# Sigmoid attention with a token-mixing MLP: 64x64 transposes for a part, PSUM as four pairs, output in half blocks

## The chip, the cores and the metric

The kernel runs on one core of a Trainium2 chip. The metric is the time of one execution on the device, in microseconds; beside it stands the span of the profiled execution, from its first to its last instruction. The engines are named as in the profile: PE is TensorE, DVE is VectorE, ACT is ScalarE, POOL is GpSimd and SP is SyncE, which issues most DMAs.

## The reference

```
# q, k, v: (8, 12, 448, 64) fp32
scores = q @ k^T / 8 - log(448)
attn = sigmoid(scores)
x = (attn @ v), heads side by side        # (8, 448, 768)
wq, wk = x @ w_q, x @ w_k                 # 768 -> 64
W_tok = (wq @ wk^T) / 8                   # (8, 448, 448)
mixed = W_tok @ x
out = relu(mixed) @ w_out                 # (8, 448, 768) fp32
```

The kernel multiplies wk^T by x first, a 64x768 matrix, and then wq by that, so that the 448x448 matrix W_tok is never made.

## The kernel before

**Groups.** The 96 heads are taken four at a time: 24 groups, three for each of the 8 batch elements u. For a group, q, k and v are loaded as fp32 by SyncE (`load1`), 448 KB each, and cast to bf16 by GpSimd (`cast1`). q and k must then stand with the 64 head dimensions on partitions. `tr` does that in one of two ways. For most groups TensorE makes seven whole-array transposes (128x128) for q and seven for k into a PSUM bank, and VectorE copies them out (L161, L165). For the groups in `TWICE`, 16 to 22, q and k are loaded nearly twice over (`qb`, `kb`, four DMAs of 216 KB each), and VectorE transposes them in 32x32 blocks from SBUF to SBUF (L154), without TensorE.

**Attention.** A group has seven score steps (`scores`, S). A step is four matmuls of 64 rows, 64 columns and 448 moving columns, one on each quarter of the array, into a pair of PSUM banks; then ScalarE takes the sigmoid of 128x896 elements (L179). Seven value steps (`values`, P), again four matmuls each, add up the group's output in one pair, which VectorE casts to the tile xt.

**MLP.** For each u: `tr_x` (x, eight whole transposes per group, evacuated to xn), `mlp_wqk` (W, six matmuls into one bank), `mlp_wkn` (N, transposes of wk), `mlp_tmp` (U, eight matmuls of 128x64), `mlp_mix` (M, four matmuls on quarters of the array, then relu). For each pair of u, `out_chunk` (O) makes 14 blocks of 128x384 output from six matmuls of 384 columns each, a copy to SBUF by VectorE (capital O) or ScalarE (small o), and a store.

**PSUM.** Eight banks are handed out by two lists. `free2` has three pairs, for scores, values and mixes; `free1` has two single banks, for everything else. Both are first in, first out, and the next user's first matmul waits until the last one's evacuation is done.

**Order.** TensorE runs in program order, and that order is written out by hand: `PLAN`, one letter for each step. Loads and casts follow the list `ORDER` as far as buffers are free (`pump_loads`, `pump`). A capital K is the second half of group 0's k; each of the 25 strings of `PLAN` but the last holds the seven score steps of a group. The array's shape is 128x128 for whole transposes, W and O, 64x64 for S, P and M, and 128x64 for U.

Of the kernel before, what the change touches and what calls it, by code (L numbers as in the profile page):

```python
# [16 lines left out]
def kernel(  # L17
# [19 lines left out]
    P = 128  # L37
# [27 lines left out]
    ps_f = pool("ps_f", 1, space=bass.MemoryType.PSUM)  # L65

    free2 = ["a", "b", "c"]
    free1 = ["d", "e"]

    def bank2(name):  # L70
        n = free2.pop(0)
        return n, ps_q.tile([P, 2, 512], F32, tag=n, name=name)

    def bank(shape, dtype, name):
        n = free1.pop(0)
        return n, ps_f.tile(shape, dtype, tag=n, name=name)
# [3 lines left out]
    wqk32 = singles.tile([P, NC, P], F32, name="wqk32")  # L80
# [4 lines left out]
    zeros = singles.tile([P, P], BF16)  # L85
# [16 lines left out]
    TWICE = {'q': (16, 17, 18, 19, 20, 21, 22), 'k': (16, 17, 18, 19, 20, 21, 22)}  # L102
# [3 lines left out]

    def load1(n, nm, eng):
        u, j = quads[n]
        if n in TWICE.get(nm, ()):
            t = p_lb.tile([P, 2, 14 * HD], F32, tag=nm + "b32", name=nm + "b32")  # L110
            for g in range(2):
                src = SRC[nm][u, 4 * j + 2 * g : 4 * j + 2 * g + 2].rearrange(
                    "h (p r) d -> p h (r d)", r=14
                )
                for dh in range(2):
                    r0 = 64 * g + 32 * dh
                    eng.dma_start(  # L117
                        out=t[r0 : r0 + 32, :, 0 : 13 * HD + 32],
                        in_=src[:, :, 32 * dh : 32 * dh + 13 * HD + 32],
                    )  # L120
        else:
            t = p_ld.tile([P, 2, NI * HD], F32, tag=nm + "32", name=nm + "32")
            eng.dma_start(  # L123
                out=t,
                in_=SRC[nm][u, 4 * j : 4 * j + 4].rearrange(
                    "(g h) (p i) d -> (h p) g (i d)", g=2, i=NI
                ),
            )
        ld[nm, n] = t

    def cast1(n, nm, eng):
        if n in TWICE.get(nm, ()):
# [5 lines left out]
        else:  # L138
            p = p_v16 if nm == "v" else p_c16
            t16 = p.tile([P, NI, 2, HD], BF16, tag=nm + "16", name=nm + "16")  # L140
            eng.tensor_copy(  # L141
                out=t16.rearrange("p i b d -> p b i d"),
                in_=ld.pop((nm, n)).rearrange("p b (i d) -> p b i d", i=NI),
            )
        ld[nm + "16", n] = t16

    qk = {}

    def tr(n, nm):
        t16 = ld.pop((nm + "16", n))  # L150
        t = p_qk.tile([P, 2, NI, NP], BF16, tag=nm + "t", name=nm + "t")
        qk[nm, n] = t
        if n in TWICE.get(nm, ()):
            nc.vector.transpose(  # L154
                out=t.rearrange("p h i n -> p (h i n)").bitcast(F32),
# [3 lines left out]
        fb, ps = bank([P, NI, 2, NP], BF16, "pt" + nm)  # L159
        for i in range(NI):  # L160
            nc.tensor.transpose(  # L161
                ps[:, i].rearrange("p h n -> p (h n)"),
                t16[:, i].rearrange("p b d -> p (b d)"), ident16,
            )
        nc.vector.tensor_copy(out=t, in_=ps.rearrange("p i h n -> p h i n"))  # L165
        free1.append(fb)
# [3 lines left out]
    def scores(n, i):  # L170
        fb, sc = bank2("sc")
        for g in range(2):
            for h in range(2):
                nc.tensor.matmul(  # L174
                    sc[HALF[h], g, 0:S], qk["k", n][HALF[g], h, i, :],
                    qk["q", n][HALF[g], h].rearrange("p i n -> p (i n)"), start=True, stop=True,
# [3 lines left out]
        free2.append(fb)  # L180
# [4 lines left out]
    def values(n, i, tail):  # L185
        u, j = quads[n]
        if i == 0:
            pv[n] = bank2("pv")
        fb, ps = pv[n]
# [6 lines left out]
        if i == NI - 1:  # L196
# [5 lines left out]
            free2.append(fb)  # L202
# [3 lines left out]
    def tr_x(n, tail):  # L206
# [3 lines left out]
        fb, ps = bank([P, 4, 2, 2, HD], BF16, "px")  # L210
        for h in range(2):
            for m in range(4):
                nc.tensor.transpose(  # L213
                    ps[:, m, :, h], xt(u, j)[:, h, m * P : (m + 1) * P], ident16
                )
        for g in range(2) if tail else (slice(0, 2),):
            w = slice(2 * j * P, 2 * (j + 1) * P) if not tail else slice((2 * j + g) * P, (2 * j + g + 1) * P)
            COPY["s" if tail and g else "v"](  # L218
                out=xns[u][:, :, w],
                in_=ps[:, :, g].rearrange("p m h d -> p m (h d)")  # L220
                if tail else ps.rearrange("p m g h d -> p m (g h d)"),
            )
        free1.append(fb)
# [4 lines left out]
    def mlp_wqk(u, c, tail):  # L228
        if c == 0:
            pw[u] = bank([P, S], F32, "pw")  # L230
        fb, ps = pw[u]
# [3 lines left out]
        if c == NC - 1:  # L235
# [6 lines left out]
            free1.append(fb)  # L242

    def mlp_wkn(u):
        fb, ps = bank([P, 4, P], BF16, "pk")
        for m in range(4):
            nc.tensor.transpose(ps[:, m], wqks[u % 2][:, m * P : (m + 1) * P], ident16)
        wkn[u] = p_one.tile([P, 4, DH], BF16, tag="wkn", name="wkn")
        nc.vector.tensor_copy(out=wkn[u], in_=ps[:, :, 64:128])
        free1.append(fb)  # L250

    def mlp_tmp(u, act):
        tmps[u] = p_one.tile([P, NB], BF16, tag="tmp", name="tmp")
        fb, ps = bank([P, NB], F32, "pt")
# [7 lines left out]
        free1.append(fb)  # L262
# [7 lines left out]
    def mlp_mix(u, c, act, tail):  # L270
        if c == 0 and u % 2 == 0:
            mxs[u // 2] = [p_mx.tile([P, 2, 2, S], BF16, tag=f"mx{n}", name="mx") for n in range(NC // 2)]
        fb, ps = bank2("pm")
# [13 lines left out]
        free2.append(fb)  # L287
# [3 lines left out]

    def out_chunk(act, tail):
        w, m, nb = chunks.pop(0)
        if nb == 0:
# [3 lines left out]
        def block(ps, w0, w1):  # L298
            for c in range(NC):
# [14 lines left out]
        fb, ps = bank([P, NB], F32, "po")  # L314
        if tail and w == NU // 2 - 1 and not chunks:
            h = NB // 2
            block(ps[:, 0:h], NB, NB + h)
            nc.vector.tensor_copy(out=o[:, NB : NB + h], in_=ps[:, 0:h])
            fb2, ps2 = bank2("po")
            block(ps2[:, 0, 0:h], NB + h, D)  # L320
            nc.scalar.copy(out=o[:, NB + h :], in_=ps2[:, 0, 0:h])
            store(slice(NB, NB + h))
            store(slice(NB + h, D))
            return
        block(ps, nb * NB, (nb + 1) * NB)
        COPY["s" if act else "v"](out=o[:, nb * NB : (nb + 1) * NB], in_=ps)  # L326
        free1.append(fb)
# [6 lines left out]
    def load_weights():  # L334
        for x, w in enumerate((moe_w_q, moe_w_k)):
            nc.sync.dma_start(
                out=wqk32[:, :, 64 * x : 64 * x + 64], in_=w.rearrange("(c p) n -> p c n", p=P)
# [20 lines left out]
    nc.vector.memset(zeros, 0.0)  # L358
    nc.vector.memset(bias_t, attn_bias)
    nc.gpsimd.memset(ident, 0.0)  # L360
# [6 lines left out]
    fb, ps = bank2("pwarm")  # L367
    for _ in range(32):
        nc.tensor.matmul(ps[:, 0, 0:P], zeros, zeros, start=True, stop=True)
    free2.append(fb)  # L370
    for t in xts:
        nc.vector.memset(t[:, :, S:], 0.0)
    for t in wqks:
# [4 lines left out]
        "v0 q1 k1 v1 k2 q2 q3 k3 q4 k4 v2 k5 k6 w0 k7 v3 "  # L378
        "w1 q5 q6 k8 v4 w2 q7 w3 v5 w4 k9 q8 v6 q9 w5 w6 "
        "v7 q10 k10 v8 v9 q11 k11 q12 v10 k12 v11 q13 k13 k14 q14 q15 "  # L380
        "v12 q16 k15 v13 v14 q17 k16 v15 k17 q18 k18 q19 v16 k19 v17 k20 "
        "k21 v18 v19 v20 v21 q20 q21 q22 v22 q23 k22 k23 v23 "
# [3 lines left out]
    BACK = {}  # L386
    for nm in "qkv":
        mine = {True: [], False: []}
        for n in range(N):
            kind = n in TWICE.get(nm, ())  # L390
            BACK[nm, n] = (kind, list(mine[kind]))
            mine[kind].append(n)

    def pump_loads():
        while len(loaded) < len(ORDER):
            nm, n = ORDER[len(loaded)]
            if nm == "w":
                if n >= 3 and ("w", n - 2) not in cast:
                    break
                load_wout(n - 1) if n else load_weights()  # L400
            else:
                kind, before = BACK[nm, n]
                back = 2 if kind else 3
# [154 lines left out]
```

## Time and profile before

| | before |
|---|---|
| median of 3 runs | 205.62 us (205.08 to 206.51) |
| the profiled execution | 204.95 us, its span 203.2 us |
| PE (TensorE) busy | 192.2 us, 95% |
| ACT (ScalarE) busy | 171.2 us, 84% |
| DVE (VectorE) busy | 123.1 us, 61% |
| POOL (GpSimd) busy | 80.3 us, 40% |
| first sigmoid of scores starts, last one ends | 6.81 us, 177.69 us |
| HBM read, written | 41.75 MB, 11.01 MB |

In the profile's rows a group of instructions stands with its source line, its engine, the tiles it writes and reads, and the shape. For TensorE, 64\*64 or 128\*128 is the part of the array in use. Matmuls are pipelined: each has a record from its start to its modelled end, and these overlap, so the time that a matmul takes from the next is seen only between starts. "Idle before" names the instruction that ended a wait.

### The profile page before, as it was taken

Reading aid. Unit: us, or ns where it says so; the run is one execution under the profiler, and the core shown is the slowest. Engines: PE = TensorE matmul, PEld = TensorE weight load, DVE = VectorE, ACT = ScalarE, POOL = GpSimd, SP = SyncE. Lnnn points to the kernel's source line nnn. Section 1 sums busy time; section 2 is a strip of 40 time slices with the busy share of each in tenths; the row PEclk is TensorE's granted clock in tenths of the full one; section 3 lists DMA queues with packets and bytes.
Section 4 is the critical chain, followed back from the end, with each engine's and each line's share of the span. In section 5 each row is a group of like instructions: output and inputs, shape, how many; then the busy total and the mean of one; then the engine's idle time right before and its main releaser. Section 6 shows DMA issues by size and latency. Waiting matters only on the chain.

```text
span 203.2 us, 5863 instructions
## 1 busy us (share of the span) xinstructions
PE 192.2 (95%) x2388; PEld 108.6 (53%) x2388; DVE 123.1 (61%) x196; ACT 171.2 (84%) x200; POOL 80.3 (40%) x95
## 2 busy tenths in 40 slices
PE   7669999999999999999999999999999899999991
PEld 7335545545556566555656555545455455555561
DVE  2226655866498567668777776858777654471230
ACT  4796999999989999889999999898998959974511
POOL 1577688676416624217642442511632600000000
PEclk9996999999999999999999999999999999999999
DMA  6999999899998999999999999999899933303575
GB/s 193 374 383 375 325 380 355 245 395 382 380 381 258 331 254 317 223 265 261 247 223 285 256 282 236 367 260 252 258 287 214 345 90 78 80 3 97 152 203 168
DMA packets 27786, 53.13 MB, mean 262 GB/s; under 512 B 4464, under 2 KB 19952, under 8 KB 27760
## 3 DMA queue, kind: packets, MB, share of 16 engines
q1 hardware_dynamic: 26960, 51.19, 85.9%
q10 hardware_dynamic: 800, 1.57, 2.1%
q8 instruction: 18, 0.29, 0.6%
q14 instruction: 8, 0.07, 0.1%
HBM read 41.75 MB, written 11.01 MB: 260 GB/s over the span
## 4 chain that ended last, share of the span: by engine, by line
DMA 41%; PE 31%; SPq 8%; ACT 8%; issue 4%; POOL 4%; DVE 1%; ACTq 1%; POOLq 0%
DMA qb<-in_q_dram 17%; DMA kb<-in_k_dram 12%; PE po L300 11%; PE sc L174 6%; ACT at L179 6%; SPq L117 5%; PE pv L192 5%; DMA q<-in_q_dram 4%; DMA out_dram<-o 4%; DMA v<-in_v_dram 4%; SPq L123 2%; PE pw L232 2%; PE ptk L161 2%; POOL k L134 2%; PE pt L257 2%
## 5 line engine op out<-in xcount | busy, mean ns | idle before, releaser
L179 ACT ACTIVATE at<-sc,bias_t 128x896 bf16<-128x896 f32 x168 | 156.1, 1016 | 13.6 <-PE sc L174 12.7
L300 PE MATMUL po<-wout,mx 128*128 128x384 bf16 (+1 forms) x342 | 61.8, 324 | 0.5 <-ACT o L326 0.3
L174 PE MATMUL sc<-qt,kt 64*64 64x448 bf16 x672 | 57.3, 363 | 2.4 <-DVE kt L451 1.0
L192 PE MATMUL pv<-at,v 64*64 64x448 bf16 x672 | 43.2, 353 | 0.7 <-POOL v L141 0.6
L300 PEld LDWEIGHTS <-mx 128*128 128x128 bf16 x342 | 30.9, 98 | 24.0 <-issue 7.0
L174 PEld LDWEIGHTS <-kt 64*64 64x64 bf16 x672 | 22.1, 104 | 24.3 <-issue 13.0
L201 DVE CAST xt<-pv 128x896 bf16<-128x896 f32 x23 | 25.0, 1088 | 16.1 <-PE pv L192 15.9
L326 DVE COPY o<-po 128x384 f32<-128x384 f32 x39 | 21.7, 556 | 16.9 <-PE po L300 11.8
L141 POOL CAST v<-v 128x896 bf16<-128x896 f32 x24 | 22.4, 934 | 15.2 <-PE pv L192 7.8
L268 DVE TENSOR_SCALAR mx<-pm 128x896 bf16<-128x896 f32 (+1 forms) x24 | 23.0, 969 | 7.2 <-PE pm L277 7.1
L192 PEld LDWEIGHTS <-v 64*64 64x64 bf16 x672 | 20.2, 107 | 12.3 <-issue 2.0
L218 DVE COPY xn<-px 128x1024 bf16<-128x1024 bf16 (+1 forms) x24 | 15.9, 663 | 7.3 <-PE px L213 7.2
L141 POOL CAST q<-q 128x896 bf16<-128x896 f32 x16 | 14.9, 933 | 9.9 <-DMA out_dram<-o 4.4
L141 POOL CAST k<-k 128x896 bf16<-128x896 f32 x16 | 14.9, 933 | 7.1 <-DMA k<-in_k_dram 4.3
L134 POOL CAST k<-kb 128x896 bf16<-128x896 f32 x7 | 8.3, 1192 | 19.4 <-DMA kb<-in_k_dram 9.2
L134 POOL CAST q<-qb 128x896 bf16<-128x896 f32 x7 | 8.2, 1190 | 18.3 <-issue 7.9
L213 PE MATMUL px<-ident,xt 128*128 128x128 bf16 x192 | 14.8, 220 | 0.1
L326 ACT COPY o<-po 128x384 f32<-128x384 f32 x16 | 7.7, 482 | 8.1 <-PE po L300 8.0
L213 PEld LDWEIGHTS <-xt 128*128 128x128 bf16 x192 | 11.5, 98 | 5.6 <-issue 4.8
L165 DVE COPY qt<-ptq 128x896 bf16<-128x896 bf16 x16 | 9.7, 618 | 7.1 <-PE ptq L161 7.0
L232 PE MATMUL pw<-xt,wqk 128*128 128x448 bf16 x48 | 13.8, 356 | 0.0
L165 DVE COPY kt<-ptk 128x896 bf16<-128x896 bf16 x16 | 9.9, 619 | 5.7 <-PE ptk L161 5.5
(53 smaller groups left out, 125.6 us busy)
## 6 DMA issues: line engine op xcount, KB each, us to landing
v<-in_v_dram SPq DMA_DIRECT2D x24, 448.0 KB, 7.8
out_dram<-o SPq DMA_DIRECT2D x47, 192.0 KB, 6.0
q<-in_q_dram SPq DMA_DIRECT2D x17, 448.0 KB, 7.5
k<-in_k_dram SPq DMA_DIRECT2D x16, 448.0 KB, 8.5
qb<-in_q_dram SPq DMA_DIRECT2D x28, 216.0 KB, 6.9
kb<-in_k_dram SPq DMA_DIRECT2D x28, 216.0 KB, 7.4
w<-in_moe_w_out_dram SPq DMA_DIRECT2D x6, 384.0 KB, 7.5
out_dram<-o ACTq DMA_DIRECT2D x7, 192.0 KB, 3.2
```

The source lines that it names most:

```text
L134: eng.tensor_copy(out=t16.rearrange("p h i d y -> p h y i d"), in_=ld.pop((nm, n)).rearrange("p h (y i d) -> p h y i d", y=2, d=HD)[..., 0 ...
L141: eng.tensor_copy(out=t16.rearrange("p i b d -> p b i d"), in_=ld.pop((nm, n)).rearrange("p b (i d) -> p b i d", i=NI),)
L165: nc.vector.tensor_copy(out=t, in_=ps.rearrange("p i h n -> p h i n"))
L174: nc.tensor.matmul(sc[HALF[h], g, 0:S], qk["k", n][HALF[g], h, i, :], qk["q", n][HALF[g], h].rearrange("p i n -> p (i n)"), start=True, st ...
L179: nc.scalar.activation(at, sc[:, :, 0:S], ACTF.Sigmoid, bias=bias_t, scale=attn_scale)
L192: nc.tensor.matmul(ps[HALF[g], h, 0:S], ld["v16", n][HALF[h], i, g, :], ats[n, i][HALF[h], g, :], start=(i == 0), stop=(i == NI - 1),)
L201: nc.vector.tensor_copy(out=xt(u, j)[:, :, 0:S], in_=ps[:, :, 0:S])
L213: nc.tensor.transpose(ps[:, m, :, h], xt(u, j)[:, h, m * P : (m + 1) * P], ident16)
L232: nc.tensor.matmul(ps, wqk16[:, c, :], xt(u, c // 2)[:, c % 2, 0:S], start=(c == 0), stop=(c == NC - 1),)
L268: nc.vector.tensor_scalar(dst, ps, moe_scale, 0.0, ALU.mult, ALU.max)
L300: nc.tensor.matmul(ps, mxs[w][c % 3][:, c // 3].rearrange("p b s -> p (b s)")[:, m * P : (m + 1) * P], wout16[:, c, w0:w1], start=(c == 0) ...
L326: COPY["s" if act else "v"](out=o[:, nb * NB : (nb + 1) * NB], in_=ps)
```

## The change

q, k and v, the casts and the arithmetic stay as they are. What changes:

- **Transposes.** A letter of `PLAN` now says how a group's q and k are transposed: a and b in the whole array, q and k in 64x64 tiles (28 matmuls each for seven), c and d by VectorE. Groups 1 to 8, 10 and 11 are of the first kind, 9, 12 to 15 and 17 of the second, 16 and 18 to 23 of the third. X is a transposition of x in the whole array, x one in 64x64 tiles (32 matmuls for eight): eight X and 16 x. wk is transposed in tiles too. q and k of a group go to one pair of banks and are evacuated by one copy.
- **PSUM.** All eight banks are four pairs. `bank2` gives a pair, `bank1` half of one; `release` joins halves again.
- **Output.** An output block is made in two steps of three matmuls each, with other work between them; of the very last block the two halves of columns are computed, copied and stored one after the other.
- **Fillers.** F is a step of four matmuls on zeros with 512 columns, into the pair that is used next; there are 15.
- **Order.** `PLAN` and `ORDER` are new; w_q and w_k are loaded through the buffers of w_out.

```diff
-    ps_f = pool("ps_f", 1, space=bass.MemoryType.PSUM)
-    free2 = ["a", "b", "c"]
-    free1 = ["d", "e"]
-    def bank2(name):
+    pairs = [ps_q.tile([P, 2, 512], F32, tag=f"pp{n}", name=f"pp{n}") for n in range(4)]
+    pairs16 = [t.rearrange("p b x -> p (b x)").bitcast(BF16).rearrange("p (b x) -> p b x", b=2) for t in pairs]
+    free2 = [0, 1, 2, 3]
+    halves = []
+    def bank2():
         n = free2.pop(0)
-        return n, ps_q.tile([P, 2, 512], F32, tag=n, name=name)
-    def bank(shape, dtype, name):
-        n = free1.pop(0)
-        return n, ps_f.tile(shape, dtype, tag=n, name=name)
+        return n, pairs[n], pairs16[n]
+    def bank1():
+        if halves:
+            n, b = halves.pop(0)
+        else:
+            n, b = free2.pop(0), 0
+            halves.append((n, 1))
+        return (n, b), pairs[n][:, b], pairs16[n][:, b]
+    def release(fb):
+        if isinstance(fb, int):
+            free2.append(fb)
+        elif (fb[0], 1 - fb[1]) in halves:
+            halves.remove((fb[0], 1 - fb[1]))
+            free2.append(fb[0])
+        else:
+            halves.append(fb)
...
-    zeros = singles.tile([P, P], BF16)
+    zeros = singles.tile([P, 512], BF16)
...
-    TWICE = {'q': (16, 17, 18, 19, 20, 21, 22), 'k': (16, 17, 18, 19, 20, 21, 22)}
...
+    PLAN = (
+        "FSSFSFKFFSFSabSSa",
+        "SbFPPSPSPSPFPPSabSFPPSP",
+        "SPabSPPSPFSabSXSSxPPP",
+        "SPPPPSSWWWSXWWSWSabSFF",
+        "SNaSbSUSPPPSMPPPSPSPPPM",
+        "SPPSPPSabSFqkSXSMSab",
+        "SSPPPPSPPPSabSWXSSWWXWP",
+        "SPPPSPPPSoOSqkSOWSWOSo",
+        "SNqkSUSOXSPMPSPPPSPPSOO",
+        "SPPxSPPPSPPSoWOSMSWWWoSFM",
+        "SWOWSFSqkOSNOSPPxSPPPPSP",
+        "SoOSUSPPqSPkPPSPPSWOSPPP",
+        "SPPPPSOWSxSOWMSWWoSMSoWO",
+        "SPPxSPcPPSPPSOOOSMSXOSPPPPNd",
+        "SPPPSUqkSSOXOSScOWOWSx",
+        "SoOWSMSOOSPPPdPSPPPSOOSM",
+        "SWoWoSMSOWOSPPxSPPPNScPPSoO",
+        "SSSoUSOOOSPPMSPPPSPP",
+        "SOOSPPdxSPPPPSPSooooMScSoO",
+        "SOOSPPMSPPPPSPSWWoSdxWoWSx",
+        "SOWOSxSoWScPdPPPPNSPPSUOS",
+        "SMOOoocxSPPMPmPPdPSPSWoWOSSSWoWWWOO",
+        "SNSOOoSxSPPPcPPdSSPPoOUSxPP",
+        "SPPPSPPSOWoWSMSWOoPPSPS",
+        "ooPPPMPMOWOWWoxxNoOooUOoOoMMmOoOooOOooOoOOooOOoo",
+    )
+    PLAN = "".join(PLAN)
+    KIND = ["a"] + [t for t in PLAN if t in "qac"]
...
+    def twice(nm, n):
+        return nm in "qk" and KIND[n] == "c"
...
+    qk = {}
+    ps_qk = {}
+    def transposes(ps, t16, r):
+        for x, i in enumerate(range(r.start, r.stop)):
+            for g in range(2):
+                for h in range(2):
+                    nc.tensor.transpose(
+                        ps[HALF[g], h, x * NP : (x + 1) * NP], t16[HALF[h], i, g, :],
+                        ident16[HALF[h], HALF[h]],
+                    )
+    def transposes_whole(ps, t16, r):
+        for x, i in enumerate(range(r.start, r.stop)):
+            nc.tensor.transpose(
+                ps[:, x * P : (x + 1) * P], t16[:, i].rearrange("p b d -> p (b d)"), ident16,
             )
...
+    def tr(n, nm, kind):
...
+        if kind in "cd":
...
-        fb, ps = bank([P, NI, 2, NP], BF16, "pt" + nm)
-        for i in range(NI):
-            nc.tensor.transpose(
-                ps[:, i].rearrange("p h n -> p (h n)"),
-                t16[:, i].rearrange("p b d -> p (b d)"), ident16,
-            )
-        nc.vector.tensor_copy(out=t, in_=ps.rearrange("p i h n -> p h i n"))
-        free1.append(fb)
+        if t == 0:
+            ps_qk[n] = bank2()
+        fb, _, ps = ps_qk[n]
+        if kind in "ab":
+            transposes_whole(ps[:, t], t16, slice(0, NI))
+        else:
+            transposes(ps[:, :, t * S : (t + 1) * S], t16, slice(0, NI))
+        if t == 1:
+            qk[n] = p_qk.tile([P, 2, 2, NI, NP], BF16, tag="qk", name="qk")
+            if kind in "ab":
+                nc.vector.tensor_copy(
+                    out=qk[n].rearrange("p t h i n -> p t i h n"),
+                    in_=ps[:, :, 0 : 2 * S].rearrange("p t (i h n) -> p t i h n", i=NI, h=2),
+                )
+            else:
+                nc.vector.tensor_copy(
+                    out=qk[n].rearrange("p t h i n -> p t h (i n)"),
+                    in_=ps[:, :, 0 : 2 * S].rearrange("p h (t x) -> p t h x", t=2),
+                )
+            release(fb)
...
-    def tr_x(n, tail):
+    def tr_x(n, tail, whole):
...
-        fb, ps = bank([P, 4, 2, 2, HD], BF16, "px")
-        for h in range(2):
-            for m in range(4):
-                nc.tensor.transpose(
-                    ps[:, m, :, h], xt(u, j)[:, h, m * P : (m + 1) * P], ident16
-                )
+        if whole:
+            fb, _, ps = bank1()
+            ps = ps.rearrange("p (m g h d) -> p m g h d", m=4, g=2, h=2)
+            for h in range(2):
+                for m in range(4):
+                    nc.tensor.transpose(
+                        ps[:, m, :, h], xt(u, j)[:, h, m * P : (m + 1) * P], ident16
+                    )
...
+        fb, _, ps = bank2()
+        for m in range(4):
+            for h in range(2):
+                for g in range(2):
+                    for c in range(2):
+                        nc.tensor.transpose(
+                            ps[HALF[c], g, (2 * m + h) * HD : (2 * m + h + 1) * HD],
+                            xt(u, j)[HALF[g], h, (2 * m + c) * HD : (2 * m + c + 1) * HD],
+                            ident16[HALF[g], HALF[g]],
+                        )
         for g in range(2) if tail else (slice(0, 2),):
...
+        release(fb)
...
     def mlp_wkn(u):
-        fb, ps = bank([P, 4, P], BF16, "pk")
+        fb, _, ps = bank1()
         for m in range(4):
-            nc.tensor.transpose(ps[:, m], wqks[u % 2][:, m * P : (m + 1) * P], ident16)
+            for c in range(2):
+                nc.tensor.transpose(
+                    ps[HALF[c], m * DH : (m + 1) * DH],
+                    wqks[u % 2][HALF[1], (2 * m + c) * DH : (2 * m + c + 1) * DH],
+                    ident16[HALF[1], HALF[1]],
+                )
...
+    opened = []
     def out_chunk(act, tail):
-        w, m, nb = chunks.pop(0)
-        if nb == 0:
+        if opened:
+            w, m, nb, fb, ps = opened.pop()
+            part = 1
+        else:
+            w, m, nb = chunks.pop(0)
+            fb, ps, _ = bank1()
+            part = 0
...
-        def block(ps, w0, w1):
-            for c in range(NC):
+        def block(ps, w0, w1, c0, c1):
+            for c in range(c0, c1):
...
-        fb, ps = bank([P, NB], F32, "po")
-        if tail and w == NU // 2 - 1 and not chunks:
+        last = w == NU // 2 - 1 and not chunks
+        if last:
             h = NB // 2
-            block(ps[:, 0:h], NB, NB + h)
-            nc.vector.tensor_copy(out=o[:, NB : NB + h], in_=ps[:, 0:h])
-            fb2, ps2 = bank2("po")
-            block(ps2[:, 0, 0:h], NB + h, D)
-            nc.scalar.copy(out=o[:, NB + h :], in_=ps2[:, 0, 0:h])
-            store(slice(NB, NB + h))
-            store(slice(NB + h, D))
+            c0 = NB + part * h
+            block(ps[:, 0:h], c0, c0 + h, 0, NC)
+            COPY["vs"[part]](out=o[:, c0 : c0 + h], in_=ps[:, 0:h])
+            release(fb)
+            store(slice(c0, c0 + h))
+            if not part:
+                opened.append((w, m, nb, *bank1()[:2]))
             return
-        block(ps, nb * NB, (nb + 1) * NB)
+        ps = ps[:, 0:NB] if not part else ps
+        block(ps, nb * NB, (nb + 1) * NB, part * NC // 2, (part + 1) * NC // 2)
+        if not part:
+            opened.append((w, m, nb, fb, ps))
+            return
...
     def load_weights():
+        w32["qk"] = p_w32.tile([P, D], F32, tag="w32", name="w32")
...
-    nc.vector.memset(zeros, 0.0)
+    nc.vector.memset(zeros[:, 0:P], 0.0)
     nc.vector.memset(bias_t, attn_bias)
+    nc.vector.memset(zeros[:, P:], 0.0)
...
-        "v0 q1 k1 v1 k2 q2 q3 k3 q4 k4 v2 k5 k6 w0 k7 v3 "
-        "w1 q5 q6 k8 v4 w2 q7 w3 v5 w4 k9 q8 v6 q9 w5 w6 "
-        "v7 q10 k10 v8 v9 q11 k11 q12 v10 k12 v11 q13 k13 k14 q14 q15 "
-        "v12 q16 k15 v13 v14 q17 k16 v15 k17 q18 k18 q19 v16 k19 v17 k20 "
-        "k21 v18 v19 v20 v21 q20 q21 q22 v22 q23 k22 k23 v23 "
+        "k1 q1 v0 q2 k2 k3 q3 v1 q4 k4 k5 q5 q6 v2 w0 k6 "
+        "w1 q7 k7 v3 q8 k8 k9 v4 w2 w3 q9 v5 q10 k10 q11 w4 "
+        "k11 w5 v6 k12 w6 v7 q12 k13 q13 q14 q15 v8 v9 k14 k15 k16 "
+        "v10 v11 k17 q16 v12 v13 q17 v14 k18 k19 q18 q19 v15 k20 v16 v17 "
+        "v18 v19 q20 v20 v21 q21 k21 q22 q23 k22 k23 v22 v23 "
...
-                if n >= 3 and ("w", n - 2) not in cast:
+                if n >= 2 and ("w", n - 2) not in cast:
...
+    qk[0] = p_qk.tile([P, 2, 2, NI, NP], BF16, tag="qk", name="qk")
+    def tr_part(nm, t16, r, e):
+        fb, _, ps = bank2()
+        transposes_whole(ps[:, 0], t16, r)
+        COPY[e](
+            out=qk[0][:, "qk".index(nm), :, r].rearrange("p h i n -> p i h n"),
+            in_=ps[:, 0, 0 : (r.stop - r.start) * P].rearrange("p (i h n) -> p i h n", h=2, n=NP),
+        )
+        release(fb)
...
-    tr_part("k", k016, KA, "v", free2[-1])
+    tr_part("k", k016, KA, "v")
...
+    ALIKE = dict(a="q", c="q", b="k", d="k", X="x")
...
+    for t in PLAN:
+        if t == "F":
+            for g in range(2):
+                for h in range(2):
+                    nc.tensor.matmul(
+                        pairs[free2[0]][HALF[h], g], zeros[HALF[g], 0:64], zeros[HALF[g], :],
+                        start=True, stop=True,
+                    )
+            continue
+        kind = ALIKE.get(t, t if t in "qkx" else t.upper())
...
-        elif t == "x":
-            tr_x(c, tail)
+        elif kind == "x":
+            tr_x(c, tail, t == "X")
```

Buffers of q and k transposed are merged into one tile `qk` for each group, and every `free1.append` and `free2.append` becomes `release`.

## The prediction

> **What bounds the kernel now.** I read the share of each engine first, then the windows of busy time cut at the first score sigmoid (6.8 us), the 49th (54.0 us) and the last (177.7 us), then the waits of ScalarE, and last TensorE's instructions in order of time, because only these say whether a busy TensorE has anything to give. The windows (TensorE, its weight loads, VectorE, ScalarE, GpSimd, granted clock, DMA share, GB/s):
>
> ```profile
> 0.00:6.80 6.80, 5.27 (x54) 4.58 (x54) 2.08 (x14) 2.57 (x4) 1.82 (x8) 1.00 0.73 234
> 6.80:54.00 47.20, 43.68 (x596) 23.54 (x592) 26.90 (x39) 44.72 (x50) 35.03 (x41) 0.96 1.02 359
> 54.00:177.70 123.70, 122.76 (x1600) 68.79 (x1593) 86.03 (x127) 113.19 (x126) 43.49 (x46) 1.00 0.93 254
> 177.70:203.20 25.50, 20.45 (x162) 11.66 (x154) 8.11 (x16) 10.70 (x22) 0.00 (x0) 1.00 0.47 124
> ```
>
> In the middle stretch TensorE is busy for 122.8 of 123.7 us, and ScalarE for 113.2. The head is near ScalarE's pace: 44.72 us for 50 sigmoids is 0.894 each, so 49 of them need 43.8 of its 47.2 us. ScalarE's waits agree that it is TensorE that is late, most of it in the middle:
>
> ```profile
> ACT at L179 <- PE sc L174: 12.7, 31, 1.5
> ```
>
> A piece of TensorE's timeline (start, time, engine, line, what) gives the price of every kind of step:
>
> ```profile
> 50.82 0.61 PE L213 MATMUL px<-ident,xt 128*128 128x128 bf16 x8
> 51.36 0.57 PE L174 MATMUL sc<-qt,kt 64*64 64x448 bf16 x8
> 51.87 1.15 PE L300 MATMUL po<-wout,mx 128*128 128x384 bf16 x6
> 52.85 0.39 PE L247 MATMUL pk<-ident,wqk 128*128 128x128 bf16 x4
> 53.17 0.38 PE L174 MATMUL sc<-qt,kt 64*64 64x448 bf16 x4
> 53.38 1.11 PE L192 MATMUL pv<-at,v 64*64 64x448 bf16 x20
> ```
>
> Each matmul's record includes a pipeline latency, so prices are taken between starts. Twenty value matmuls take 1.11 us and four alone 0.35 (mean 353 ns): five steps of four, 0.19 us a step, the four running side by side. A whole-array transpose costs (0.61-0.22)/7 = 0.056, an output matmul (1.15-0.33)/5 = 0.163. Changing the array's shape costs too: eight transposes from 50.82 would end at 51.27, but the scores begin at 51.36 (0.09); two score steps end at 51.74, and the output begins at 51.87 (0.13). So 0.11 per switch.
>
> A check on the middle: the order of instructions there has 253 steps of four (scores, values, mixes; 48.1 us), 39 output blocks of six (38.1), 30 token-weight matmuls (0.19 each, 5.7), 37 sets of whole transposes (14.6), 6 products with wkn (four pairs of 0.163, 3.9) and 101 switches (11.1). The sum is 121.5; the stretch took 123.7. TensorE's own work accounts for all but 2.2 us, so the middle can get shorter only by less TensorE work, down to ScalarE's demand.
>
> The head loses time in one place, which ScalarE's rows in order of time show:
>
> ```profile
> 13.20 1.90 ACT L179 ACTIVATE at<-sc,bias_t 128x896 bf16<-128x896 f32 x2
> 16.19 1.01 ACT L179 ACTIVATE at<-sc,bias_t 128x896 bf16<-128x896 f32 x1 [1.09 <-PE sc L174]
> 17.38 1.01 ACT L179 ACTIVATE at<-sc,bias_t 128x896 bf16<-128x896 f32 x1 [0.18 <-PE sc L174]
> 18.75 1.01 ACT L179 ACTIVATE at<-sc,bias_t 128x896 bf16<-128x896 f32 x1 [0.37 <-PE sc L174]
> 20.26 11.78 ACT L179 ACTIVATE at<-sc,bias_t 128x896 bf16<-128x896 f32 x13 [0.51 <-PE sc L174]
> ```
>
> with TensorE's rows beside them:
>
> ```profile
> 15.07 0.56 PE L161 MATMUL ptq<-ident,q 128*128 128x128 bf16 x7 [1.33 <-POOL q L141]
> 16.73 0.59 PE L174 MATMUL sc<-qt,kt 64*64 64x448 bf16 x4
> ```
>
> and the page's line of the granted clock, in 40 slices:
>
> ```profile
> PEclk9996999999999999999999999999999999999999
> ```
>
> TensorE, in order, stands behind the third group's q transposes, which wait for GpSimd's cast; then the clock line shows 0.6 in the fourth slice (15 to 20 us), and a score step takes 0.59 instead of 0.38. ScalarE's idle there adds up to 2.15 us.
>
> **The change, part by part.** Of 462 whole-array transposes, 218 stay (20 sets of seven for q and k, 14 of group 0, eight sets of eight for x). Six q/k pairs and 16 x sets become 64x64 transposes, 28 or 32 matmuls where there were seven or eight; wkn's four become eight. With four of them on the array's four quarters as one group (two for wkn), that is 244 groups: 26 in the head, 198 in the middle, 20 in the tail. VectorE still transposes seven groups (16 and 18 to 23, was 16 to 22).
>
> The unknown is c, the time of such a group, since no small matmul in 64x64 tiles runs now. Lower bound: 448 columns take 189 ns and a transpose of 128 takes 56, which is 0.416 ns a column, so 64 columns take 29 ns if four run side by side like the scores. Upper bound: the four one after another at a whole transpose's pace, 224 ns. The nearest row is the score step, whose four matmuls start together, so I stay near the low end. The first score step after a switch is longer by some 0.02 us (0.38 where one that follows a tiled step has 0.36), which I read as weight loads that nothing hides; with half of that in each group I take 40 ns.
>
> A rule against this change stands in the Trainium skill, TensorEngine Tiling (Array Packing), Instruction Overhead: every matmul has about 60 cycles of overhead, and no tiling factor should come from a dimension that is already small. Sixty cycles of 2.4 GHz are 25 ns, an estimate from that page; were the four paid one after another, c would be 100 ns and the sum below would end 13 us higher. The row shows four matmuls of a tiled step side by side, but only at 448 columns.
>
> Middle, after: 256 steps of four (48.6), 80 half output blocks of 0.489 (39.1), 35 token-weight matmuls (6.7), 6 wkn products (3.9), three whole x sets (1.3), two fillers (0.4) come to 100.0; 198 groups at 40 ns add 7.9, 99 switches 10.9 (output in halves adds switches, tiled transposes between scores take as many away). With the same 2.2 left over: 121.0, which is 2.7 less than 123.7. With c at 29 ns it is 4.9 less, at 56 ns 0.5 more. ScalarE's floor there, 119 x 0.894 and ten output copies of 0.482 and one relu of about 0.9, is 112.1, so TensorE stays the bound.
>
> Head: TensorE has about 39 us of work in 47.2. Fifteen fillers F, 13 of them here, cost 0.22 each (512 columns) and lie in that slack; without it they are 2.9 us on the path. k1 and q1 are now loaded and cast before v0, q2 is cast fourth after k0 instead of sixth, and values start later. But q2's transposes now stand ahead of the 8th score step and k2's, still the fifth cast, ahead of the 9th, where everything queued on TensorE waits for GpSimd: k2's cast ended at 13.81, and with its transposes, a filler and two value steps behind it the 9th step comes near 15 us, about 1 us after ScalarE could take it. Of the 3.4 us between 47.2 and 43.8 I take half, -1.7; the ends are -3.4 and +1.
>
> Tail: 32 half blocks (15.6), 12 steps and token-weight matmuls (2.3), one wkn product (0.65), 20 groups (0.8), nine switches (1.0) are 20.4; before, 15 blocks, 19 such steps, the transposes and seven switches are 20.9. So -0.5. The last block's first half is stored before its second is computed, so one ScalarE DMA issue of 0.50 comes off behind the last copy; the SyncE issues beside it may hide it: -0.3.
>
> PSUM: scores, values, mixes, q/k and tiled x sets take pairs, the rest halves, all from four pairs where there were three and two single banks. In the order of instructions 43 score steps wait for VectorE, 27 before; behind each stand all later matmuls, and ScalarE waits for them. VectorE has slack (86 of 123.7 us), so I add 0.6 for them. One evacuation of q and k together (two of 0.62 before) leaves VectorE's sum alone. The bytes of all loads, GpSimd's casts and SyncE's issues are as many as before; but DMA is busy at 0.93 to 1.02 until the loads end, and group 23 now has the doubled loads. If these come later than the middle's gain allows, the last seven steps wait; the loads' end near 160 us leaves some 10 us, so nothing is charged.
>
> Sum: -1.7 - 2.7 - 0.5 - 0.3 + 0.6 = -4.6, from the profiled span of 203.2 to 198.6. That execution took 204.95, 1.75 more than its span, and the median of the runs is 0.67 above it: 205.62 - 4.6 = 201.0 us.
>
> **The rivals.** (1) The tiled transposes can't be fed. A group is eight TensorE instructions, and one stretch of the new order has 167 matmuls in seven score steps, where 60 to 80 us now has 283 in 20 us. The densest run shown, 20 value matmuls, passes one in 47 ns, which makes 190 for a group. If one group in four falls to that pace, c is 78 on average, and 218 groups outside the head add 8.3: +3.7, or 209.3 us. It decides from c = 61 ns, where the gain is gone. For it: no row shows a faster pace over more than 20. Against it: four tiled matmuls do start together, which is also why the far end, c = 224 ns and 241 us, is left out of the range. (2) Nothing is won: c is 56 ns as in the whole array and the head's stall stays (q2 still waits for GpSimd). Then 0 + 0.5 - 0.1 - 0.3 + 0.6 = +0.7: 206.3 us. (3) The pairs run short: if each of the 16 added waits for VectorE costs half of a copy of 1.09 us, 8.7 us come back instead of 0.6, and the time is 209.1.
>
> **How the numbers follow.** Forecast 0.52, rival (1) 0.22, rival (2) 0.16, rival (3) 0.10. One per cent is about what this measurement tells from no change. The forecast is over 1% faster for any c below 50 ns, rival (2) is within, (1) and (3) are slower: 0.52, 0.16, 0.32. The likeliest's own range is 197.5 (c at 29 and most of the head's 3.4) to 203.5; the range reaches to 210.5, past (1) and (3).
>
> **What would show it.** Right: a tiled q set's 28 matmuls pass in 0.3 to 0.4 us between starts; the granted clock keeps 1.0 from 10 to 20 us; the 49th sigmoid ends near 52 us and the 168th near 173; TensorE is still busy throughout the middle. Wrong: sets of 28 that take over 0.45 us, or ScalarE idle behind score steps whose releaser is a VectorE copy.

## The result, and the profile after

The changed kernel takes 220.92 us (median; 218.87 to 223.81), the kernel before 205.35 beside it: 1.071 times as long, 95% interval 1.062 to 1.081. The forecast was 201.0. Ratios in this text are formed from undisturbed runs alone, so they can differ a little from the ratio of two medians.

The profiled execution took 218.87 us with a span of 217.1. The windows, cut at the first sigmoid, near the 50th and at the end of the last (same columns as before):

```profile
6.42:54.78 48.36, 42.57 (x734) 25.51 (x730) 27.23 (x30) 44.99 (x49) 36.90 (x44) 1.00 1.04 366
54.78:190.90 136.12, 123.23 (x2137) 65.49 (x2133) 83.47 (x116) 115.59 (x130) 41.81 (x45) 1.00 0.84 226
190.90:217.10 26.20, 19.06 (x208) 11.08 (x199) 10.09 (x20) 8.41 (x18) 0.00 (x0) 0.99 0.49 130
```

The time went into the middle. TensorE is busy for 123.2 us there, as before, but the stretch has grown from 123.7 to 136.1. The clock line shows that it is not the clock, whose dip in the fourth slice is even gone:

```profile
PEclk9999999999999999999999999999999999999999
```

The groups (busy time and mean ns, then the idle time before them and what ended most of it) and the waits (total us, count, longest) name the lines. L422 makes output blocks, L339 token weights; their lines in the kernel before are L300 and L232:

```profile
L262 ACT ACTIVATE at<-pp,bias_t 128x896 bf16<-128x896 f32 x168 | 156.5, 1010 | 23.7 <-PE pp L257 21.0
L422 PE MATMUL pp<-wout,mx 128*128 128x384 bf16 (+1 forms) x342 | 65.2, 324 | 9.0 <-DVE wqk L344 3.0
L339 PE MATMUL pp<-xt,wqk 128*128 128x448 bf16 x48 | 15.2, 353 | 7.0 <-DVE o L452 3.6
```

```profile
PE pp L339 <- DVE o L452: 3.6, 5, 0.9
PE pp L422 <- DVE wqk L344: 3.0, 4, 0.8
PE pp L422 <- DVE tmp L374: 2.2, 4, 0.7
PE pp L422 <- DVE xn L303: 1.9, 2, 1.1
PE pp L339 <- DVE xn L303: 1.9, 3, 0.8
PE pp L422 <- DVE wkn L361: 1.6, 3, 0.7
```

Read the pairs of names. A token-weight matmul (L339) waits for the copy of an output block (L452); an output half (L422) waits for the copy of wqk, tmp, xn or wkn. Neither reads what that copy writes. The order of instructions is the compiled program's list of what each engine runs and which waits are recorded for it. In it, with the PSUM place of each, 35 TensorE steps wait for an evacuation of the *other half* of the pair that they write. Before, TensorE stood idle ahead of outputs for 0.5 us in all and ahead of token-weight matmuls not at all:

```profile
L300 PE MATMUL po<-wout,mx 128*128 128x384 bf16 (+1 forms) x342 | 61.8, 324 | 0.5 <-ACT o L326 0.3
L232 PE MATMUL pw<-xt,wqk 128*128 128x448 bf16 x48 | 13.8, 356 | 0.0
```

One such wait in the changed kernel, in TensorE's and VectorE's rows:

```profile
29.36 0.62 PE L298 MATMUL pp<-ident,xt 128*128 128x128 bf16 x8
30.09 0.69 DVE L303 COPY xn<-pp 128x1024 bf16<-128x1024 bf16 x1 [1.10 <-PE pp L298]
30.83 0.54 PE L339 MATMUL pp<-xt,wqk 128*128 128x448 bf16 x2 [0.85 <-DVE xn L303]
31.30 0.38 PE L257 MATMUL pp<-qk 64*64 64x448 bf16 x4
```

The token weights sit in half 0 of `pp0`, the x transposes in half 1. The weight matmul stands until VectorE has copied half 1, and the score step behind it, for which ScalarE is idle, stands too.

For a sum over the whole trace I took, from each TensorE step to the next, what the step's columns (at 0.416 ns) and a change of array shape account for, and called what is left over 0.12 us a stall. After 20 us:

| kernel | stalls, us (gaps) | before outputs | before token weights | before scores |
|---|---|---|---|---|
| before | 3.8 (12) | 0.9 | 0 | 1.5 |
| after | 24.1 (38) | 10.7 | 8.6 | 2.5 |

And by stretches (starts of the 50th and the last sigmoid as cuts; TensorE's own work and the rest):

| kernel | to the 50th | middle = own work + rest | from the last on | span |
|---|---|---|---|---|
| before | 54.0 | 122.7 = 121.4 + 1.3 | 26.5 | 203.2 |
| after | 54.8 | 135.2 = 118.6 + 16.5 | 27.1 | 217.1 |

TensorE's own work in the middle did fall, by 2.8 us. The rest swallowed it five times over.

### The profile page after: what moved, and what is told of

Same layout as the page of the kernel before. It is cut to its first block, busy times and chain, and to the rows that moved or that the text cites. A ratio compares the mean times of both kernels' runs of the same rounds, so it can differ in the third digit from the quotient of the medians.

```text
span 217.1 us, 7368 instructions
## 1 busy us (share of the span) xinstructions
PE 190.2 (88%) x3116; PEld 106.5 (49%) x3116; DVE 123.1 (57%) x181; ACT 171.6 (79%) x199; POOL 79.9 (37%) x95
## 4 chain that ended last, share of the span: by engine, by line
PE 55%; DMA 22%; DVE 8%; ACT 4%; POOL 3%; issue 3%; SPq 2%; ACTq 1%; DVEq 0%; POOLq 0%
PE pp L422 22%; PE pp L257 11%; PE pp L275 10%; DMA k<-in_k_dram 8%; DMA v<-in_v_dram 7%; DMA out_dram<-o 5%; PE pp L339 4%; ACT at L262 4%; DMA q<-in_q_dram 3%; DVE mx L381 2%; PE pp L315 2%; PE pp L370 2%; SPq L174 2%; PE pp L390 2%; PE pp L215 1%
## 5 line engine op out<-in xcount | busy, mean ns | idle before, releaser
L262 ACT ACTIVATE at<-pp,bias_t 128x896 bf16<-128x896 f32 x168 | 156.5, 1010 | 23.7 <-PE pp L257 21.0
L422 PE MATMUL pp<-wout,mx 128*128 128x384 bf16 (+1 forms) x342 | 65.2, 324 | 9.0 <-DVE wqk L344 3.0
L257 PE MATMUL pp<-qk 64*64 64x448 bf16 x672 | 61.8, 361 | 1.6 <-issue 1.3
L422 PEld LDWEIGHTS <-mx 128*128 128x128 bf16 x342 | 30.7, 97 | 36.3 <-issue 20.1
L275 PE MATMUL pp<-at,v 64*64 64x448 bf16 x672 | 45.6, 350 | 0.1
L257 PEld LDWEIGHTS <-qk 64*64 64x64 bf16 x672 | 23.2, 104 | 31.9 <-issue 24.1
L452 DVE COPY o<-pp 128x384 f32<-128x384 f32 x39 | 21.7, 556 | 21.9 <-PE pp L422 19.6
L284 DVE CAST xt<-pp 128x896 bf16<-128x896 f32 x23 | 25.0, 1086 | 13.1 <-PE pp L275 10.8
L381 DVE TENSOR_SCALAR mx<-pp 128x896 bf16<-128x896 f32 (+1 forms) x23 | 22.6, 988 | 13.9 <-PE pp L390 10.4
L339 PE MATMUL pp<-xt,wqk 128*128 128x448 bf16 x48 | 15.2, 353 | 7.0 <-DVE o L452 3.6
L193 POOL CAST k<-k 128x896 bf16<-128x896 f32 x16 | 14.9, 932 | 11.4 <-PE pp L207 5.3
L240 DVE COPY qk<-pp 128x1792 bf16<-128x1792 bf16 x10 | 10.9, 1092 | 10.1 <-PE pp L215 7.1
L452 ACT COPY o<-pp 128x384 f32<-128x384 f32 x16 | 7.7, 481 | 6.0 <-PE pp L422 4.2
```

Source lines behind the costliest of these rows:

```text
L193: eng.tensor_copy(out=t16.rearrange("p i b d -> p b i d"), in_=ld.pop((nm, n)).rearrange("p b (i d) -> p b i d", i=NI),)
L240: nc.vector.tensor_copy(out=qk[n].rearrange("p t h i n -> p t i h n"), in_=ps[:, :, 0 : 2 * S].rearrange("p t (i h n) -> p t i h n", i=NI, ...
L257: nc.tensor.matmul(sc[HALF[h], g, 0:S], qk[n][HALF[g], 1, h, i, :], qk[n][HALF[g], 0, h].rearrange("p i n -> p (i n)"), start=True, stop=True,
L262: nc.scalar.activation(at, sc[:, :, 0:S], ACTF.Sigmoid, bias=bias_t, scale=attn_scale)
L275: nc.tensor.matmul(ps[HALF[g], h, 0:S], ld["v16", n][HALF[h], i, g, :], ats[n, i][HALF[h], g, :], start=(i == 0), stop=(i == NI - 1),)
L284: nc.vector.tensor_copy(out=xt(u, j)[:, :, 0:S], in_=ps[:, :, 0:S])
```

## The experiments

Theory A: the loss is the waits between the two halves of a pair, because each pair is one tile and the waits are recorded for a whole tile. Rivals: four pairs are truly too few (B in e1), or the tiled transposes or the clock are the loss (C).

**e1: the same instructions, PSUM as one tile of eight banks.** For one tile that spans all of PSUM the waits in the order of instructions come out bank by bank; for tiles of two banks they do not, and stand for the whole tile.

```diff
-    pairs = [ps_q.tile([P, 2, 512], F32, tag=f"pp{n}", name=f"pp{n}") for n in range(4)]
+    psum = ps_q.tile([P, 8, 512], F32, tag="psum", name="psum")
+    pairs = [psum[:, 2 * n : 2 * n + 2] for n in range(4)]
```

> The changed kernel with its four PSUM pairs declared as slices of one tile of eight banks instead of four tiles of two banks; every instruction is the same. In the changed kernel 35 TensorE steps wait for the evacuation of the other half of their pair (16 of them output halves, 14 token-weight matmuls); with one tile of eight banks the recorded waits are bank by bank and token-weight matmuls that wait fall from 19 to 7. Theory A (these cross-half waits are the loss): TensorE's stalls after 20 us fall from 24.1 us in 38 gaps to 4 to 6 us, and the time from 220.9 to 199 to 203 us. Theory B (four pairs are truly too few, the waits only move to another evacuation): over 214 us. Theory C (the tiled transposes or the clock are the loss): 219 to 222.

Measured: 203.72 us (200.11 to 207.85), ratio to before 0.982 (0.972 to 0.991); profiled span 200.1, stalls 6.9 us. The ratio is formed from two of its ten executions; the medians of all, 203.72 and 205.65, are 0.9% apart. The same place as above:

```profile
29.55 0.62 PE L299 MATMUL psum<-ident,xt 128*128 128x128 bf16 x8
30.01 0.54 PE L340 MATMUL psum<-xt,wqk 128*128 128x448 bf16 x2
30.28 0.69 DVE L304 COPY xn<-psum 128x1024 bf16<-128x1024 bf16 x1 [1.27 <-PE psum L299]
30.48 0.38 PE L258 MATMUL psum<-qk 64*64 64x448 bf16 x4
```

The weight matmuls now run before VectorE has even begun its copy of the other half. In the groups the idle time of both lines is gone, and ScalarE's is 10.0 us instead of 23.7:

```profile
L263 ACT ACTIVATE at<-psum,bias_t 128x896 bf16<-128x896 f32 x168 | 156.7, 1012 | 10.0 <-PE psum L258 8.6
L423 PE MATMUL psum<-wout,mx 128*128 128x384 bf16 (+1 forms) x342 | 65.1, 324 | 0.0
L340 PE MATMUL psum<-xt,wqk 128*128 128x448 bf16 x48 | 15.4, 355 | 0.3
```

Theory A held, though not quite with its numbers (stalls of 4 to 6 us, 199 to 203 us); B (over 214) and C (219 to 222) fall.

**e8: e1 again,** because e1's times were spread.

> The one-tile version (e1) once more and with more rounds, because its first times were spread from 200.1 to 207.9 us. Theory A (the changed kernel without its cross-half waits gains what TensorE saves, 3 us on the profiled spans): 201 to 203.5 us, 1 to 2% under the kernel before. Theory B (e1 was only a lucky execution): 204.5 to 207.

Measured: 204.32 us (201.18 to 208.89), ratio 0.991 (0.987 to 0.995), span 201.1. The median lies between the two expected ranges, and 0.2% under the 204.81 of the kernel before beside it; the ratio says 0.9%. So the change without its cross-half waits is some 17 us faster than the changed kernel, far beyond the spread, but against the kernel before the gain is small and its size not settled: 0.9% and 0.2% by the medians of e1 and e8, 1.8% and 0.9% by the ratios.

**e2: the reverse, in the kernel before.** Its banks d and e become the halves of one tile.

```diff
-    free1 = ["d", "e"]
+    free1 = [0, 1]
+    two = ps_f.tile([P, 2, 512], F32, tag="two", name="two")
...
-        return n, ps_f.tile(shape, dtype, tag=n, name=name)
+        ps = (two if dtype == F32 else two16)[:, n, 0 : math.prod(shape[1:])]
...
```

> The kernel before with its two single banks d and e declared as the two halves of one tile; everything else as before. The order of instructions then has about 130 TensorE steps that wait for the evacuation of the other bank. Theory A: each that is not hidden costs some 0.6 us, as in the changed kernel (24.1 us over 35 such waits), so the time rises by 20 to 70 us, to 225 to 275 us, with the stalls ahead of output, token-weight and transpose steps. Theory B or C (cross-half waits are harmless): 204 to 208 us.

Measured: 269.01 us, ratio 1.317 (1.300 to 1.334); stalls 71.7 us, 39.1 of them ahead of outputs. Its waits are of the same kinds:

```profile
PE two L309 <- DVE xn L227: 6.8, 8, 1.5
PE two L309 <- ACT o L335: 5.2, 8, 1.3
PE two L309 <- DVE o L335: 4.7, 7, 0.7
PE two L241 <- DVE xn L227: 3.4, 4, 1.0
```

Neither a tiled transpose nor an output half is in this kernel: sharing a tile is enough by itself.

**e7: the kernel before in one tile of eight banks,** with its three pairs and two singles as slices of `psum`, as the control for e1.

> The kernel before with its three pairs and two single banks declared as slices of one tile of eight banks; every instruction is the same. It has no cross-half waits on TensorE; but in the tail VectorE and ScalarE copy the two halves of one pair, and these two copies are in turn recorded as waiting for each other. Theory A (e1 wins because its cross-half waits are gone, not because one tile is better in itself): 203 to 206 us, at most the tail shorter by 1 to 2 us. Theory B (one tile of eight banks speeds up any kernel): 198 to 202 us, as much as e1.

Measured: 204.28 us, ratio 0.999 (0.995 to 1.002). Theory A: one tile is no gain where no two steps had shared a tile by halves.

**e3: output in whole blocks again, four tiles kept.** The first half of a block does nothing, the second computes all six matmuls.

```diff
-        block(ps, nb * NB, (nb + 1) * NB, part * NC // 2, (part + 1) * NC // 2)
+        block(ps, nb * NB, (nb + 1) * NB, 0, NC)
```

> The changed kernel with output blocks of six matmuls again, at the place of each second half; all else as in the changed kernel, its four PSUM pairs included. 23 cross-half waits are left of 35, 18 of them token-weight matmuls and 3 output blocks. Theory A: the loss of 24.1 us shrinks about with their number, to 16 us, so about 211 to 215 us. If the halves themselves (array switches, an output block held open) were the loss: 201 to 206 us. If neither: 219 to 222.

Measured: 218.02 us, ratio 1.063 (1.052 to 1.075). This missed. I had scaled the loss with the number of waits (23 of 35), but the stalls are still 24.2 us: ahead of outputs 4.2 instead of 10.7, ahead of token weights 9.2 instead of 8.6, ahead of scores 5.4 instead of 2.5. A count of waits is not a price: the waits that go leave others to come last.

**e6: the same whole blocks on one tile,** so the halves by themselves.

> The one-tile version (e1) with output blocks of six matmuls at the place of each second half; the last block of all stays in two stored halves. With no cross-half waits the halves are priced by themselves: they add 5 array switches (0.5 us) and cut the lumps of 1 us in front of the scores into two of 0.5. Theory A (halves are worth nothing by themselves): within 1 us of e1. Theory B (shorter lumps keep ScalarE fed): 1.5 to 4 us over e1. Theory C (the switches decide): 1 us or more under e1.

Measured: 207.66 us, ratio 1.016 (1.006 to 1.025); stalls 13.8 us, against 6.9 and 7.9 in e1 and e8. So theory B: with waits by bank the halves gain 3 to 4 us by the medians of e6, e1 and e8, and 5 to 7 by the ratios. With waits by tile (e3 against the changed kernel) whole blocks were 2.9 us better by the medians, but the two intervals, 1.052 to 1.075 and 1.062 to 1.081, overlap. So the wait took the gain of this part of the change away; that it turned it into a loss is not shown.

**e4: the transposes in the whole array, on one tile,** q to a, k to b and x to X throughout PLAN.

> The one-tile version (e1) with every transpose of q, k and x on TensorE back in the whole array (wkn's stay tiled), at the same places. By 0.056 us a whole transpose and 33 ns a tiled group, 12 q and k sets and 16 x sets take 4.9 us more, and each set that lay between steps of the 64x64 shape adds two switches of about 0.11 us, 2 to 5 us together. If the tiled transposes are worth what the prediction's price said: 6 to 10 us over e1. If they cannot be fed (rival 1): e4 faster than e1 by some us. If they are worth nothing: within 1.5 us of e1.

Measured: 214.79 us, ratio 1.047 (1.032 to 1.062), 11 us over e1. TensorE's columns are 4.6 us more and its switches 4.3 (186 instead of 151), the stalls 2.9 more. These 11.8 us are most of the 13.9 between the two profiled spans; e4's granted clock was 0.975 there and e1's 0.998, so a part of the rest may be the clock's. Tiled transposes pay, by a little more than expected.

**e10: three pairs and two single banks, on one tile.**

```diff
-    free2 = [0, 1, 2, 3]
-    halves = []
+    free2 = [0, 1, 2]
+    halves = [(3, 0), (3, 1)]
...
-        elif (fb[0], 1 - fb[1]) in halves:
+        elif fb[0] != 3 and (fb[0], 1 - fb[1]) in halves:
```

> The one-tile version (e1) with the banks divided as in the kernel before: three pairs, and the fourth pair's two banks for single-bank steps alone; the order of steps is the changed kernel's. Theory A (the order does not lean on the fourth pair; only the recorded cross-half waits mattered): within 1.5 us of e1. Theory B (four pairs that any step may take are worth something): 2 to 8 us over e1, with ScalarE's or VectorE's evacuations as releasers of the score steps.

Measured: 221.99 us, ratio 1.085 (1.080 to 1.091). Theory B, and far past its range: 18 us over e1. Here the score steps' waits in the trace are true ones, for the sigmoid that still reads the pair, and ScalarE in turn waits for the scores:

```profile
ACT at L263 <- PE psum L258: 22.1, 47, 1.2
PE psum L258 <- ACT at L263: 6.4, 13, 0.6
```

The changed order, with its tiled q, k and x sets that take pairs, needs the fourth pair; it is the recording of waits that spoiled it.

**e5: no fillers, on one tile.**

> The one-tile version (e1) without its fifteen filler groups F, which compute nothing that is used; all else as in e1. The fillers take about 0.22 us each, 13 of them where TensorE has slack. Theory A (hidden in slack, and the clock does not depend on them): within 0.8 us of e1. Theory B (they hold the granted clock): the dip to 0.6 near 15 to 20 us comes back, score steps there take 0.59 us, and the time is 0.8 to 2 us over e1. Theory C (they stand in the way): 1 to 3 us under e1.

Measured: 206.41 us, ratio 1.010 (1.001 to 1.019), 2.7 us over e1 by the medians. The dip is back: the clock, 1.00 in both of these windows in e1, is 0.58 and 0.74 here (the third number from the end):

```profile
10.00:15.00 5.00, 4.42 (x44) 2.61 (x48) 1.20 (x2) 3.99 (x5) 3.73 (x4) 0.58 1.06 382
15.00:20.00 5.00, 5.00 (x74) 2.81 (x70) 2.67 (x3) 3.90 (x5) 3.42 (x4) 0.74 1.05 378
```

So the fillers do hold the clock. But the dip delays the 22nd sigmoid by 0.45 us (27.70 against 27.24 in e1) and the 50th not at all (53.26 against 53.54): from 16 us to the 50th ScalarE is idle for 0.65 us in e1 and for 0.21 in e5, which makes up for it. The time was lost elsewhere: 3.28 us at 78 us, in one stall that nothing released:

```profile
81.54 0.76 PE L276 MATMUL psum<-at,v 64*64 64x448 bf16 x11 [3.28 <-issue]
```

Without it the span of 203.8 would be within half a microsecond of e1's. Whether that stall comes in every execution is open: the profiled one was the fastest of four, and the others have no trace.

**e9: every set of groups 1 to 8 and of x tiled, on one tile.**

> The one-tile version (e1) with the remaining whole-array transposes of groups 1 to 8 and of x also in 64x64 tiles (group 0 stays whole). By e4, tiling 12 q and k sets and 16 x sets is worth 9 us of TensorE work, some 0.3 us a set with its two switches; 18 more q and k sets and a few x sets are 6 to 7 us less work. Theory A: most of them lie in the first 54 us, where ScalarE is the bound, so 0 to 3 us under e1, 199 to 202.5 us. Theory B (the emptier array loses its clock in the first 20 us, or the transposes' many instructions come late): 0 to 4 us over e1.

Measured: 217.87 us, ratio 1.062 (1.055 to 1.069), 14 us over e1: past the worst case expected. By the 50th sigmoid it is 11 us late (64.5 against 53.5), with stalls like that of e5 in the midst of transposes:

```profile
27.03 0.32 PE L208 MATMUL psum<-ident,k 64*64 64x64 bf16 x15 [2.57 <-issue]
39.97 0.22 PE L356 MATMUL psum<-ident,wqk 64*64 64x64 bf16 x2 [1.76 <-issue]
52.09 0.23 PE L208 MATMUL psum<-ident,q 64*64 64x64 bf16 x5 [2.54 <-issue]
```

TensorE waits for nothing that the profile shows, while it has many short instructions to run. Three more such stalls, of 0.75, 1.10 and 2.37 us, end at 33.50, 61.46 and 74.04 us; the six make 11.1 of the 13.0 us between the profiled spans of e9 and e1. I come back to them in the last section. The clock dips too (0.6 to 0.7 in three slices before 60 us), so not all of the loss need be these stalls.

## Why the prediction was wrong, point by point

**The step that failed is the PSUM term, +0.6.** It priced waits of score steps for VectorE (43, 27 before), and of nothing else. The waits that cost stand one step earlier in TensorE's queue: 19 token-weight steps wait for VectorE or ScalarE where seven did, and output halves, held open across other steps, wait for copies of their neighbour's half. The same order of instructions listed them. I took the halves of a pair for banks that come free singly, since the allocator hands them out so, and did not look at whose evacuation each step waits for. In place of +0.6: about 15 us in the middle (16.5 of rest against 1.3). With the declaration alone, e1 takes 12.5 of them away (its rest is 4.0), and e2 produces such waits, 71.7 us of stalls, in the kernel before.

**The middle, -2.7, was right as TensorE's work and wrong as time.** Own work fell from 121.4 to 118.6 us. The price c of a group of four was, if anything, high: between 62.11 and 62.68 us, from the first transpose to the next score step, 64 tiled transposes pass in 0.57 us, 8.9 ns each and 36 ns a group, against 40 assumed.

```profile
62.22 0.36 PE L207 MATMUL pp<-ident,q 64*64 64x64 bf16 x21
62.45 0.41 PE L207 MATMUL pp<-ident,k 64*64 64x64 bf16 x26
62.68 0.38 PE L257 MATMUL pp<-qk 64*64 64x448 bf16 x4
```

The other tiled sets of this trace ahead of the tail pass in 7.8 to 11.4 ns a transpose. So a set of 28 takes some 0.25 us, under the 0.3 to 0.4 that was to show the forecast right. The Trainium skill, TensorEngine Tiling (Array Packing), Instruction Overhead, states about 60 cycles for each matmul, which the prediction made 25 ns, an estimate. Paid one after another over the four quarters that would be 100 ns a group; these rows show 36, so here the four quarters overlap. The 36 ns from one matmul of a quarter to the next lie above 25, so these rows don't contradict the figure itself. But the assumption "with the same 2.2 left over" fails even without the shared tiles: e1's middle is 118.4 + 4.0 = 122.4 us, so the 3.0 us less work became 0.3 us less time. In the profiled execution of e8, the same kernel, the middle took 124.1 us, 1.4 more than before. With TensorE less full, small waits (values and scores for evacuations, one stall of 1.1 us at issue) took the rest. So in neither of these two does the saving of the middle arrive as time.

**The head, -1.7, was over-sized.** The clock stayed at 1.0, as forecast, and the 22nd sigmoid starts at 27.30 us instead of 28.29. Two waits of token-weight matmuls for the copy of xn gave that back, the one at 30 us shown above and one that ends at 53.82 us; behind them ScalarE stood idle for 0.79 and 1.10 us. The 50th starts at 54.78, 0.8 later than before. In e1 0.46 us of gain is left there.

**The tail and the end, -0.8 together:** +0.7 in the changed kernel, and -2.3 in e1 (24.2 us against 26.5). Cross-half waits stood in the tail too; without them it was worth more than I gave it.

Together, after against before: +0.8, +12.5 and +0.7 make up the 13.9 us between the spans, but for rounding. e1: -0.46, -0.3 and -2.3 make up its -3.0, where the forecast's sum was -4.6.

**The rivals.** (1) was wrong at this place: c is 36, not 78. The stalls of e9 in the midst of tiled sets may be its mechanism, where more sets are packed into the first 54 us; their cause is not shown. (2) is excluded by e4: on one tile, tiling is worth 11 us. (3) had the nearest mechanism, pairs and VectorE's copies, but the wrong steps, scores for want of a pair, and so too small a price. Of the signs named for right, three failed: TensorE is not busy throughout the middle, the 49th sigmoid ends at 53.7 us and not near 52, and the 168th at 190.9 and not near 173 (53.7 and 176.9 in e1). Neither sign named for wrong came: the sets are short, and score steps stood behind output and token-weight matmuls that waited, not behind a VectorE copy of their own.

## What to carry to other kernels

When a change lets several steps share one buffer, list for every step which instruction it waits for and where in the buffer the two touch; if they touch different parts, that wait is one of bookkeeping, and in the groups shown above it took 0.5 to 1.0 us each time on average, on an engine that runs in order. Before giving up such a change, try the declaration that lets the waits be recorded for the parts; here two lines took 17 us back, and one part (the output halves), which had gained nothing, was worth 3 to 4 us. And a count of waits, in either direction, is no price: take the stalls from the trace and ask what comes last when one is gone.

## What the hardware showed that was not expected

TensorE's long stalls at issue go with packets of its instruction stream. The page's DMA queues list "q8 instruction" with 18 packets (0.29 MB) before, 24 (0.39 MB) after and 29 (0.48 MB) in e9, 16 KB each; 0.39 MB over the 6,238 matmuls and weight loads that the trace of the changed kernel has is 63 bytes each, and the same division gives 62 before and 64 in e9, so I read this as that engine's code. In the trace's records of that queue, one packet ends 1.4 to 1.5 us ahead of the end of each of these stalls:

| kernel | packet, us | stall, us | from the packet's end to the stall's |
|---|---|---|---|
| after | 70.50 to 71.56 | 71.77 to 73.03 | 1.47 |
| e5 | 78.88 to 80.00 | 78.26 to 81.54 | 1.54 |
| e9 | 24.33 to 25.62 | 24.46 to 27.03 | 1.41 |
| e9 | 37.38 to 38.52 | 38.21 to 39.97 | 1.45 |
| e9 | 49.64 to 50.60 | 49.54 to 52.09 | 1.48 |

Nine more stalls of 0.75 to 2.37 us in the traces of e1, e3, e6, e8, e9 and e10 end 1.27 to 1.69 us after such a packet. In the kernel before, and in e2, e4 and e7, whose sets of q, k and x are whole, no such stall reaches 0.6 us. Most packets are followed by none: of the changed kernel's 24, one is. That code arriving late is the cause fits all of these but was not tested by itself. The Trainium skill, Runtime: NRT & Kernel Launch, Instruction fetch mechanics, says that code is refilled in 16 KiB blocks, which these packets agree with, and that the cost of crossing into the next block is mostly hidden. If these stalls are that crossing, it was not hidden there, at up to 3.28 us.

The same skill's PSUM page (PSUM — Partial Sum Buffer, the section on bank collisions) asks for guards by bank and quadrant, or by bank as the simple version. The changed kernel's waits were by pairs of banks, coarser than that, and e1's are by bank.
